# Unused matmuls during the first attention batch, a projection moved into the head pairs, and two casts moved to ScalarE, in a fused attention and MLP kernel

## The chip, the cores and the metric

The kernel runs on one core of one Trainium2 chip. The metric is the device time in microseconds (us) of one execution. Six executions of the kernel before had a median of 781.19 us (779.12 to 784.26).

Five engines appear in the profile, each with its own list of instructions, and they work side by side: in a span of 777.3 us PE was busy for 708.0 us and DVE for 336.0. PE is TensorE, which multiplies matrices. PEld is PE's loading of weights. DVE is VectorE, ACT is ScalarE, and POOL is GpSimd, which here mostly issues the loads from memory (DMA; 126 of its 140 instructions in the kernel before). The traces of that kernel show instructions that wait for what they read (0.74 us for `av` matmuls at 65.29) and for the buffer that they write (0.74 us for scores at 72.67, until the exponential before had read it). What stood behind a waiting instruction in its list waited too; the traces below show this for DVE (9.93 us).

## The reference

```python
# batch 8, heads 12, sequence 448, head_dim 64, d_model 768, rank 32
q_n = q / (norm(q, axis=-1) + 1e-6)
k_n = k / (norm(k, axis=-1) + 1e-6)
attn = softmax(q_n @ k_n.T / tau)            # tau = 0.1
x = heads_merged(attn @ v)                   # (8, 448, 768)
xt = x.transpose(0, 2, 1)
u = x + (xt @ U @ V).transpose(0, 2, 1)      # = (I + U V).T applied along the sequence
out = u + relu(u @ w_ch1) @ w_ch2            # w_ch1 768 x 3072, w_ch2 3072 x 768
```

## The kernel before

Work is organised by batch. `emit_attention(b)` loads and normalises q and k, then goes through six pairs of heads. `emit_mlp(b)` projects with `I + UV` (`pu`), then does the two large products `ph` (24 blocks of 6 matmuls) and `pc` (6 blocks of 24), transposes back (`po`) and stores. The program lists attention(0), attention(1), mlp(0), attention(2), mlp(1) and so on. The build turns that into one fixed order of instructions for each engine. In the middle of the run this order puts the matmuls of the MLP between those of the next attention, so PE has something to do (for 84.92 of 87.17 us in the period shown below). During attention(0) there is no MLP work yet.

The parts that matter here, cut:

```python
nc.vector.tensor_copy(out=u_nat_bf, in_=u_nat)     # two small casts, on DVE
...
nc.vector.tensor_copy(out=v_bf, in_=v_nat)
...
def emit_attention(b):
    ...                                   # 12 loads on the POOL queue: q (4), k (4), v (4)
    for w_, src, sc in ((0, q_bf, tau_f), (1, k_bf, 1.0)):
        for t in range(NT):               # NT = 4
            nc.vector.tensor_tensor(out=sq, in0=src[:, t], in1=src[:, t], op=ALU.mult)
            nc.vector.reduce_sum(out=ssq[:, w_, t], in_=sq, axis=mybir.AxisListType.X)
        nc.scalar.activation(out=nrm[:, w_], in_=ssq[:, w_], func=AF.Sqrt,
                             bias=sqrt_bias[:PT], scale=sc * sc)
        nc.vector.reciprocal(out=rcp[:, w_], in_=nrm[:, w_])
        ...                               # four multiplies on DVE: src *= rcp
    for p in range(NP):                   # NP = 6 pairs of heads
        ...                               # transposes of q and k into tp_ps; copy to tp_sb
        for jt in range(NT):
            sc_ps = psum.tile([PT, 2, 512], F32, name="sc_ps", tag="sc", bufs=1)
            ...                           # two score matmuls
            ex = apool.tile([PT, 2, S], BF16, name="ex", bufs=5)
            nc.scalar.activation(out=ex, in_=sc_ps[:, :, :S], func=AF.Exp)
        for hh in range(2):
            ...                           # av: 16 matmuls ex x v into av_ps (tag "av", bufs=2)
            ...                           # DVE: x = av / row sum
        for _ in range(3):                # 3 of the 30 weight loads, on the POOL queue
            ...
def emit_mlp(b):
    for cc in range(NC):
        pu = psum.tile([128, S], F32, name="pu", tag="mm", bufs=3)
        ...                               # 4 matmuls x x (I + UV); copy to uT
    ...                                   # ph -> relu, pc + uT -> oT, po -> ost -> out
```

There is one score buffer, so a score matmul has to wait until the exponential of the previous one has read it (0.92 us for each exponential; steps of 1.69 us in the slow attention(0) of the kernel before, at 71 to 74 us). I call the time from one score to the next a step; a pair has four.

## Time and profile before

| stage of the profiled run (span 777.3 us) | start, us | what limits it |
|---|---|---|
| load and normalise batch 0 | 0 | loads |
| attention(0), alone | 28 | slow array, score and exponential in turn, one stop for a load |
| attention(1) with `ph` of batch 0 | 100.50 | PE |
| `pc` of batch 0; from here about 86.5 us per batch | 156.57 | PE |
| last batch and tail | 708 | PE |

The head of the profile page gives each engine's busy time, then the busy tenths in 40 equal slices of the span (9 means 90% or more), then the share of each engine in the chain of work that ended last:

```profile
PE 708.0 (91%) x5000; PEld 388.8 (50%) x5000; DVE 336.0 (43%) x620; ACT 310.4 (40%) x399; POOL 108.5 (14%) x140
...
PE   1547799999999999999999999999999999999995
...
PEclk9999999999999999999999999999999999999998
DMA  9999983772099029342198029522000010002002
```

PE is the bottleneck, but only from the sixth slice on. Two thirds of PE's idle time, 46 of 69 us, lie in the first five slices, that is, the first 100 us. A mean of 91% hides that.

From the chain of waits in order of time (start, duration, what; all in us):

```profile
50.85 7.61 DMA q_bf<-in_q_dram
...
156.57 27.24 PE pc L220 x144
...
243.50 27.24 PE pc L220 x144
...
708.19 3.31 PE pu L192 x16
711.50 27.24 PE ph L206 x144
738.74 27.25 PE pc L220 x144
```

The starts of `pc` are a ruler. From one to the next is one batch, 86.93 us here. The load of q at 50.85 is on the chain because something had to stop for it. The stretch table shows how tight a period is, and how tight the start is not. Its columns are the stretch and its length, the busy time and count of PE, PEld, DVE, ACT and POOL, the granted clock, the DMA share and GB/s:

```profile
330.74:417.91 87.17, 84.92 (x625) 46.46 (x624) 43.52 (x80) 36.72 (x46) 11.44 (x13) 1.00 0.46 40
60.00:84.00 24.00, 19.19 (x108) 11.10 (x108) 17.01 (x31) 15.03 (x18) 13.96 (x21) 1.00 2.14 155
```

Now the start, instruction by instruction, from PE's timeline (start, duration, engine, line, operation, output<-inputs, shapes, count, and in brackets the idle time before and what ended it):

```profile
48.26 0.62 PE L147 MATMUL sc_ps<-tp_sb 64*112 64x448 bf16 x2
...
59.43 0.56 PE L192 MATMUL pu<-pt_sb,x 112*128 112x448 bf16 x1 [10.06 <-DVE x L170]
...
65.29 2.64 PE L162 MATMUL av_ps<-v_sb,ex 112*112 112x65 bf16 x26 [0.74 <-ACT ex L154]
...
104.58 1.70 PE L206 MATMUL ph<-uT,w 128*128 128x448 bf16 x4
...
109.26 1.11 PE L206 MATMUL ph<-uT,w 128*128 128x448 bf16 x5
110.28 1.53 PE L162 MATMUL av_ps<-v_sb,ex 112*112 112x65 bf16 x26
```

The same 26 `av` matmuls take 2.64 us at 65.29 and 1.53 us at 110.28. The array ran slow throughout attention(0), although the clock row shows 9 everywhere: from 60 to 84 us PE was busy for 19.19 of 24 us, and two scores took 0.62 us there. It became fast in the dense `ph` matmuls, about 4 us after they begin: they start at 104.58, and from 108.81 on two scores take 0.40 us. And PE stood still for 10.06 us. DVE's timeline shows why:

```profile
58.48 0.56 DVE L119 TENSOR_TENSOR sq<-q_bf 112x768 bf16<-112x768 bf16 x1 [9.93 <-DMA q_bf<-in_q_dram]
58.96 0.42 DVE L170 TENSOR_TENSOR x<-av_ps,rs 112x256 bf16<-112x256 f32 x1
```

The multiply that PE needed (`x`) had its inputs long before. But a square of batch 1's q stood ahead of it in DVE's queue, and that square waited for its load.

### The profile page before, as it was taken

The page shows a single profiled execution, that of the slowest core. Times are in us where ns is not written, and L with a number is a line of the kernel's source. Part 1 is how long each engine was busy: PE and PEld are TensorE (multiplying, and loading weights), DVE is VectorE, ACT ScalarE, POOL GpSimd, SP SyncE. Part 2 cuts the span into 40 slices and gives each one's busy share as a digit, 9 for nine tenths or more (in the row PEclk, how much of TensorE's full clock was granted, in tenths as well). Part 3 has the DMA queues.
Part 4 walks back from the last instruction along what each step waited for, and adds up shares of the span by engine and source line. Part 5 has one row for each costly group of instructions (what it writes and reads, how often), then busy time and mean ns, then how long its engine had stood idle before and what let it go on. Part 6 is the DMA issues. An engine that isn't in the chain of part 4 may idle for free.

```text
span 777.3 us, 11607 instructions
## 1 busy us (share of the span) xinstructions
PE 708.0 (91%) x5000; PEld 388.8 (50%) x5000; DVE 336.0 (43%) x620; ACT 310.4 (40%) x399; POOL 108.5 (14%) x140
## 2 busy tenths in 40 slices
PE   1547799999999999999999999999999999999995
PEld 0324455555555554555545555555555555554552
DVE  7418665933484155913484156813430153111011
ACT  2325557613563065603563056603552155303401
POOL 6355422110122003100122003100000000000000
PEclk9999999999999999999999999999999999999998
DMA  9999983772099029342198029522000010002002
GB/s 114 184 200 147 134 36 26 48 36 71 3 70 36 1 72 72 23 14 72 8 66 36 1 72 72 30 7 72 1 2 1 21 51 1 1 1 72 1 0 72
DMA packets 139539, 37.82 MB, mean 49 GB/s; under 512 B 132032, under 2 KB 135136, under 8 KB 139488
## 3 DMA queue, kind: packets, MB, share of 16 engines
q0 software_dynamic: 134880, 25.96, 48.7%
q1 hardware_dynamic: 4608, 11.13, 4.6%
q8 instruction: 39, 0.64, 0.4%
q14 instruction: 12, 0.10, 0.0%
HBM read 52.02 MB, written 11.01 MB: 81 GB/s over the span
## 4 chain that ended last, share of the span: by engine, by line
PE 76%; DMA 10%; ACT 6%; DVE 3%; POOL 2%; issue 2%; SPq 0%; ACTq 0%; POOLq 0%; DVEq 0%
PE pc L220 28%; PE ph L206 22%; PE av_ps L162 11%; PE sc_ps L147 7%; PE pu L192 4%; DMA q_bf<-in_q_dram 4%; DMA w<-in_moe_w_ch_dram 3%; ACT ex L154 3%; DMA v_sb<-in_v_dram 1%; POOL q_bf L106 1%; ACT L154 1%; PE tp_ps L137 1%; PE po L233 1%; PE tp_ps L135 1%; DVE ssq L120 1%
## 5 line engine op out<-in xcount | busy, mean ns | idle before, releaser
L206 PE MATMUL ph<-uT,w 128*128 128x448 bf16 x1152 | 245.7, 354 | 0.0
L154 ACT ACTIVATE ex<-sc_ps 112x896 bf16<-112x896 f32 x192 | 176.0, 917 | 154.6 <-PE sc_ps L147 152.6
L220 PE MATMUL pc<-relu,w 128*128 128x448 bf16 x1152 | 219.2, 352 | 0.0
L220 PEld LDWEIGHTS <-w 128*128 128x128 bf16 x1152 | 112.7, 98 | 105.2
L206 PEld LDWEIGHTS <-w 128*128 128x128 bf16 x1152 | 105.8, 100 | 88.9 <-issue 10.9
L227 DVE TENSOR_TENSOR oT<-pc,uT 128x448 bf16<-128x448 f32 x48 | 30.0, 624 | 239.5 <-PE pc L220 239.5
L162 PE MATMUL av_ps<-v_sb,ex 112*112 112x65 bf16 x1536 | 125.2, 228 | 8.6 <-DVE x L170 5.7
L162 PEld LDWEIGHTS <-ex 112*112 112x112 bf16 x1536 | 102.7, 141 | 47.4 <-issue 32.5
L236 ACT CAST ost<-po 112x768 f32<-112x768 bf16 x17 | 13.6, 798 | 225.4 <-PE po L233 221.3
L147 PE MATMUL sc_ps<-tp_sb 64*112 64x448 bf16 x384 | 82.2, 420 | 8.4 <-ACT ex L154 7.3
L213 ACT ACTIVATE relu<-ph 128x448 bf16<-128x448 f32 x120 | 65.1, 542 | 49.2 <-PE ph L206 49.1
L213 DVE TENSOR_SCALAR relu<-ph 128x448 bf16<-128x448 f32 x72 | 44.6, 619 | 42.4 <-PE ph L206 41.8
L192 PE MATMUL pu<-pt_sb,x 112*128 112x448 bf16 x192 | 50.5, 380 | 11.6 <-DVE x L170 10.2
L106 POOL DMA_DIRECT2D q_bf<-in_q_dram x32 | 30.0, 944 | 221.0 <-PE ph L206 199.4
L147 PEld LDWEIGHTS <-tp_sb 64*112 64x112 bf16 x384 | 28.2, 129 | 63.9 <-issue 58.1
L120 DVE TENSOR_REDUCE ssq<-sq 112x12 f32<-112x768 bf16 x64 | 59.2, 939 | 0.3
L110 POOL DMA_DIRECT2D v_sb<-in_v_dram x32 | 29.8, 937 | 107.2 <-issue 92.8
L140 DVE COPY tp_sb<-tp_ps 128x896 bf16<-128x896 bf16 x39 | 24.3, 623 | 46.4 <-PE sc_ps L147 32.8
L137 PE MATMUL tp_ps<-ident,k_bf 112*128 112x112 bf16 x192 | 31.3, 229 | 11.7 <-DVE k_bf L125 11.7
L170 DVE TENSOR_TENSOR x<-av_ps,rs 112x256 bf16<-112x256 f32 x96 | 39.6, 418 | 1.8
L135 PE MATMUL tp_ps<-ident,q_bf 112*128 112x112 bf16 x192 | 31.0, 227 | 9.8 <-DVE q_bf L125 5.6
L169 DVE RECIPROCAL rs<-av_ps 112x4 f32<-112x4 f32 x96 | 17.3, 180 | 45.4 <-PE av_ps L162 44.5
(37 smaller groups left out, 338.6 us busy)
## 6 DMA issues: line engine op xcount, KB each, us to landing
out_dram<-ost SPq DMA_DIRECT2D x32, 336.0 KB, 3.0
q_bf<-in_q_dram POOLq DMA_DIRECT2D x32, 168.0 KB, 5.4
k_bf<-in_k_dram POOLq DMA_DIRECT2D x32, 168.0 KB, 6.5
v_sb<-in_v_dram POOLq DMA_DIRECT2D x32, 168.0 KB, 6.6
w<-in_moe_w_ch_dram POOLq DMA_DIRECT2D x6, 768.0 KB, 13.0
w<-in_moe_w_ch_dram POOLq DMA_DIRECT2D x24, 192.0 KB, 7.6
u_nat<-in_moe_U_dram SPq DMA_DIRECT2D x1, 56.0 KB, 2.0
v_nat<-in_moe_V_dram SPq DMA_DIRECT2D x1, 56.0 KB, 2.4
```

Source lines behind the costliest of these rows:

```text
L106: nc.gpsimd.dma_start(out=q_bf[:, t], in_=qr[:, t])
L120: nc.vector.reduce_sum(out=ssq[:, w_, t], in_=sq, axis=mybir.AxisListType.X)
L135: nc.tensor.transpose(tp_ps[:, 0, t * PT:(t + 1) * PT], q_bf[:, t, 2 * p:2 * p + 2, :], ident[:PT, :PT])
L137: nc.tensor.transpose(tp_ps[:, 1, t * PT:(t + 1) * PT], k_bf[:, t, 2 * p:2 * p + 2, :], ident[:PT, :PT])
L147: nc.tensor.matmul(sc_ps[:, hh, :S], tp_sb[base:base + 64, 1, jt * PT:(jt + 1) * PT], tp_sb[base:base + 64, 0, :], start=True, stop=True,)
L154: nc.scalar.activation(out=ex, in_=sc_ps[:, :, :S], func=AF.Exp)
L162: nc.tensor.matmul(av_ps[:, ic, :], aw[jt][:, hh, ic * PT:(ic + 1) * PT], v_sb[:, jt, h, :], start=(jt == 0), stop=(jt == NT - 1),)
L170: nc.vector.tensor_tensor(out=xt[:, :, h, :], in0=av_ps[:, :, 1:], in1=rs[:, :, None].to_broadcast([PT, NT, D]), op=ALU.mult,)
L192: nc.tensor.matmul(pu, xt[:, t, 2 * cc:2 * cc + 2, :], pt_sb[t], start=(t == 0), stop=(t == NT - 1),)
L206: nc.tensor.matmul(ph, w1_sb[cc][:, fc * 128:(fc + 1) * 128], uT[cc], start=(cc == 0), stop=(cc == NC - 1),)
L213: nc.any.tensor_scalar_max(out=rl, in0=ph, scalar1=0.0)
L220: nc.tensor.matmul(pc, w2_sb[fc][:, cc * 128:(cc + 1) * 128], relu[fc], start=(fc == 0), stop=(fc == NF - 1),)
```

## The change

The intent is to win back the start and the batch changes. Unused matmuls (`dm`) in attention(0) are to keep the array fast. `pu` moves from the head of the MLP into each pair of heads, where it uses the `av` buffers instead of the `mm` buffers. Two small casts go from DVE to ACT, and `ex` gets a sixth buffer. The diff, cut to its core (the rest splits `emit_attention` into a prologue and a function per pair; the order of calls is the same):

```diff
-    nc.vector.tensor_copy(out=u_nat_bf, in_=u_nat)
+    nc.scalar.copy(out=u_nat_bf, in_=u_nat)
...
-    nc.vector.tensor_copy(out=v_bf, in_=v_nat)
+    nc.scalar.copy(out=v_bf, in_=v_nat)
...
+            if b == 0 and jt > 0:
+                dm = psum.tile([PT, S], F32, name="dm", tag="mm", bufs=3)
+                for _ in range(5):
+                    nc.tensor.matmul(dm, aw[-1][:, 0, :PT], aw[-1][:, 1, :], start=True, stop=True)
-                ex = apool.tile([PT, 2, S], BF16, name="ex", bufs=5)
+            ex = apool.tile([PT, 2, S], BF16, name="ex", bufs=6)
...
+        pu = psum.tile([128, S], F32, name="pu", tag="av", bufs=2)      # at the end of each pair
+        for t in range(NT):
+            nc.tensor.matmul(pu, xp[:, t, :, :], pt_sb[t], start=(t == 0), stop=(t == NT - 1))
+        ut = mpool.tile([128, S], BF16, name=f"uT_{p}", bufs=3)
+        nc.any.tensor_copy(out=ut, in_=pu)
...
-            pu = psum.tile([128, S], F32, name="pu", tag="mm", bufs=3)  # at the start of the MLP
-            ...
-            ut = mpool.tile([128, S], BF16, name=f"uT_{cc}", bufs=1)
```

More of the change, by code (lines that the diff above doesn't have):

```diff
@@ L41 @@
     tau_f = float(tau)
-    assert S == NT * PT and C == NC * 128 and F == NF * 128 and H % 2 == 0
+    assert S == NT * PT and C == NC * 128 and F == NF * 128 and H % 2 == 0 and NC == NP
     const = ctx.enter_context(tc.tile_pool(name="const", bufs=1))
     wpool = ctx.enter_context(tc.tile_pool(name="wpool", bufs=1))
-    xpool = ctx.enter_context(tc.tile_pool(name="xpool", bufs=1))
     apool = ctx.enter_context(tc.tile_pool(name="apool", bufs=1))
@@ L91, with emit_attention_prologue @@
     w_loads = w_loads[::-1]
-    x_sb = {}
-    def emit_attention(b):
-        xt = xpool.tile([PT, NT, H, D], BF16, name=f"x_{b % 2}", bufs=1)
-        x_sb[b] = xt
+    batch_ctx = {}
+    uT_all = {b: [None] * NP for b in range(B)}
+    def emit_attention_prologue(b):
         q_bf = apool.tile([PT, NT, H, D], BF16, name="q_bf", bufs=2)
@@ L130, in emit_attention @@
                 )
-        for p in range(NP):
-            tp_ps = psum.tile([128, 2, S], BF16, name="tp_ps", tag="tp", bufs=1)
-            for t in range(NT):
-                nc.tensor.transpose(tp_ps[:, 0, t * PT:(t + 1) * PT],
-                                    q_bf[:, t, 2 * p:2 * p + 2, :], ident[:PT, :PT])
-                nc.tensor.transpose(tp_ps[:, 1, t * PT:(t + 1) * PT],
-                                    k_bf[:, t, 2 * p:2 * p + 2, :], ident[:PT, :PT])
-            tp_sb = apool.tile([128, 2, S], BF16, name="tp_sb", bufs=2)
-            nc.any.tensor_copy(out=tp_sb, in_=tp_ps)
-            aw = []
-            for jt in range(NT):
-                sc_ps = psum.tile([PT, 2, 512], F32, name="sc_ps", tag="sc", bufs=1)
-                for hh in range(2):
-                    base = hh * 64
+        batch_ctx[b] = (q_bf, k_bf, v_sb)
@@ new lines, in emit_attention_pair @@
+    def emit_attention_pair(b, p):
+        q_bf, k_bf, v_sb = batch_ctx[b]
+        tp_ps = psum.tile([128, 2, S], BF16, name="tp_ps", tag="tp", bufs=1)
+        for t in range(NT):
+            nc.tensor.transpose(tp_ps[:, 0, t * PT:(t + 1) * PT],
+                                q_bf[:, t, 2 * p:2 * p + 2, :], ident[:PT, :PT])
+            nc.tensor.transpose(tp_ps[:, 1, t * PT:(t + 1) * PT],
+                                k_bf[:, t, 2 * p:2 * p + 2, :], ident[:PT, :PT])
+        tp_sb = apool.tile([128, 2, S], BF16, name="tp_sb", bufs=2)
+        nc.any.tensor_copy(out=tp_sb, in_=tp_ps)
+        aw = []
+        for jt in range(NT):
+            sc_ps = psum.tile([PT, 2, 512], F32, name="sc_ps", tag="sc", bufs=1)
+            for hh in range(2):
+                base = hh * 64
+                nc.tensor.matmul(
+                    sc_ps[:, hh, :S],
+                    tp_sb[base:base + 64, 1, jt * PT:(jt + 1) * PT],
+                    tp_sb[base:base + 64, 0, :],
+                    start=True, stop=True,
+                )
+            if b == 0 and jt > 0:
[3 more added lines that the diff above has]
+            ex = apool.tile([PT, 2, S], BF16, name="ex", bufs=6)
+            nc.scalar.activation(out=ex, in_=sc_ps[:, :, :S], func=AF.Exp)
+            aw.append(ex)
+        xp = apool.tile([PT, NT, 2, D], BF16, name="xp", bufs=3)
+        for hh in range(2):
+            h = 2 * p + hh
+            av_ps = psum.tile([PT, NT, D + 1], F32, name="av_ps", tag="av", bufs=2)
+            for ic in range(NT):
+                for jt in range(NT):
@@ L147, in emit_attention @@
                     nc.tensor.matmul(
-                        sc_ps[:, hh, :S],
-                        tp_sb[base:base + 64, 1, jt * PT:(jt + 1) * PT],
-                        tp_sb[base:base + 64, 0, :],
-                        start=True, stop=True,
-                    )
-                ex = apool.tile([PT, 2, S], BF16, name="ex", bufs=5)
-                nc.scalar.activation(out=ex, in_=sc_ps[:, :, :S], func=AF.Exp)
-                aw.append(ex)
-            for hh in range(2):
-                h = 2 * p + hh
-                av_ps = psum.tile([PT, NT, D + 1], F32, name="av_ps", tag="av", bufs=2)
-                for ic in range(NT):
-                    for jt in range(NT):
-                        nc.tensor.matmul(
-                            av_ps[:, ic, :],
-                            aw[jt][:, hh, ic * PT:(ic + 1) * PT],
-                            v_sb[:, jt, h, :],
-                            start=(jt == 0), stop=(jt == NT - 1),
-                        )
-                rs = apool.tile([PT, NT], F32, name="rs", bufs=3)
-                nc.vector.reciprocal(out=rs, in_=av_ps[:, :, 0])
-                nc.vector.tensor_tensor(
-                    out=xt[:, :, h, :],
-                    in0=av_ps[:, :, 1:],
-                    in1=rs[:, :, None].to_broadcast([PT, NT, D]),
-                    op=ALU.mult,
-                )
@@ L177, in emit_attention @@
-            for _ in range(3):
-                if w_loads:
-                    wt, wsrc = w_loads.pop()
-                    nc.gpsimd.dma_start(out=wt, in_=wsrc)
-        if b == 1:
-            while w_loads:
+                        av_ps[:, ic, :],
+                        aw[jt][:, hh, ic * PT:(ic + 1) * PT],
+                        v_sb[:, jt, h, :],
+                        start=(jt == 0), stop=(jt == NT - 1),
+                    )
+            rs = apool.tile([PT, NT], F32, name="rs", bufs=3)
@@ new lines, in emit_attention_pair @@
+            nc.vector.reciprocal(out=rs, in_=av_ps[:, :, 0])
+            nc.vector.tensor_tensor(
+                out=xp[:, :, hh, :],
+                in0=av_ps[:, :, 1:],
+                in1=rs[:, :, None].to_broadcast([PT, NT, D]),
+                op=ALU.mult,
+            )
+        pu = psum.tile([128, S], F32, name="pu", tag="av", bufs=2)
+        for t in range(NT):
+            nc.tensor.matmul(
+                pu,
+                xp[:, t, :, :],
+                pt_sb[t],
+                start=(t == 0), stop=(t == NT - 1),
+            )
@@ L183, in emit_attention @@
+        ut = mpool.tile([128, S], BF16, name=f"uT_{p}", bufs=3)
+        nc.any.tensor_copy(out=ut, in_=pu)
+        uT_all[b][p] = ut
+        for _ in range(3):
+            if w_loads:
                 wt, wsrc = w_loads.pop()
@@ L186, in emit_mlp @@
     def emit_mlp(b):
-        xt = x_sb.pop(b)
-        uT = []
-        for cc in range(NC):
-            pu = psum.tile([128, S], F32, name="pu", tag="mm", bufs=3)
-            for t in range(NT):
-                nc.tensor.matmul(
-                    pu,
-                    xt[:, t, 2 * cc:2 * cc + 2, :],
-                    pt_sb[t],
-                    start=(t == 0), stop=(t == NT - 1),
-                )
-            ut = mpool.tile([128, S], BF16, name=f"uT_{cc}", bufs=1)
-            nc.any.tensor_copy(out=ut, in_=pu)
-            uT.append(ut)
+        del batch_ctx[b]
+        uT = uT_all.pop(b)
         relu = []
@@ L237, in emit_mlp, with flush_w_loads @@
             nc.sync.dma_start(out=out[b, t * PT:(t + 1) * PT, :], in_=ost)
-    LAG = min(1, B - 1) if B > 1 else 1
-    if B == 1:
-        emit_attention(0)
+    def flush_w_loads():
         while w_loads:
@@ L244 @@
             nc.gpsimd.dma_start(out=wt, in_=wsrc)
+    if B == 1:
+        emit_attention_prologue(0)
+        for p in range(NP):
+            emit_attention_pair(0, p)
+        flush_w_loads()
         emit_mlp(0)
     else:
-        for step in range(B + LAG):
-            if step < B:
-                emit_attention(step)
-            if step >= LAG:
-                emit_mlp(step - LAG)
+        for b in range(B):
+            emit_attention_prologue(b)
+            for p in range(NP):
+                emit_attention_pair(b, p)
+            if b == 1:
+                flush_w_loads()
+            if b >= 1:
+                emit_mlp(b - 1)
+        emit_mlp(B - 1)
 _INS = ['q', 'k', 'v', 'tau', 'moe_U', 'moe_V', 'moe_w_ch1', 'moe_w_ch2']
```

## The prediction

> **What bounds the kernel now.** The page gives PE 708.0 of 777.3 us, 91%; the chain of waits is 76% PE. Two regimes hide in that average.
>
> - Steady state. In the chain, the second MLP product (pc) starts at 156.57, 243.50, 330.74, 417.91, 504.52, 590.57 and 675.68 us: about 86.5 us per batch. By the stretch table PE is busy 84.9 of 87.2 us. The list of waits shows only 0.6 to 2.2 us of PE idle per period (av on x 0.8 to 1.5; transposes on tp_sb 0.5; po on ost 0.2). Matmuls stream at 27.24 us / 144 = 189 ns. There is little to win.
> - Start. pc of batch 0 starts only at 156.57. From 28.0 to 100.5 us attention(0) runs alone: 72.5 us for six pairs, against about 7.4 us per pair later. By the PE timeline, three things cost this: (a) the array is slow: a pu matmul takes 374 ns, a score pair 0.62 instead of 0.40 us, 26 av matmuls 2.64 instead of 1.5 us. It turns fast only at 108.8 us, 4 us after the dense ph matmuls begin. [...]the granted-clock column already reads 1.00 there. (b) PE idles 10.06 us before 59.43: an x multiply on DVE stands behind batch 1's first square, which waits for q until 58.46, the load being queued after 18 weight loads. (c) One score buffer: matmul and exp (0.92 us) alternate, 1.69 us per step.
>
> **What the change does.**
>
> 1. 18 x 5 = 90 unused matmuls in attention(0): 17 us at 189 ns, 34 us slow. In the fast state five (0.95 us) fit under one exp: the steady state runs five ph matmuls per step at 1.49 us. In the slow state they stretch a step from 1.69 to about 2.5 us, but then fill PE for several us, so I expect the fast state within the first pair, lost in the DMA stall, regained after it.
> 2. pu moves from the MLP's start into each pair (buffers of av instead of mm). Count unchanged; the scheduler already ran batch 0's pu per pair. It removes the pu wait chain at batch changes (0.7 us each) and in the last batch, where 8.4 us pass between pc(6) and ph(7) for 4.5 us of pu and about 1.5 of po. Risk: a third user of two av buffers and a new x-to-pu wait in the attention chain.
> 3. Two casts go to ACT (0.6 us off DVE), and a sixth ex buffer: nothing on the chain.
>
> **Sum.** Attention(0): p0 and p1 get faster, but the stall until 58.5 us remains, only longer, since weights and q are DMA-bound (DMA 9 tenths until 60 us). After it, 41 us become about 31: pairs of 7.5 us, with DVE (batch 1's normalisation, about 20 us) nearly full. Gain 10 us. Ph(0) starts fast: 3 us. Batch changes: 3 us. Last batch: 2 us. New stalls: -2 us. Total about 16 us: 765 us.
>
> Predicted 765 us, 80% range 751 to 777. Faster by over 2%: 0.52; within 2%: 0.45; slower: 0.03.
>
> **What would show it.** av x26 at about 1.5 us before 60 us; pc(0) starting near 143 (plus 4.5 us for pu(1) now done before it: 148); a PE gap of 10 to 15 us ending near 59; the period still 86 to 87 us; ph(7) directly after po(6).
>
> **What would make it wrong.** The dummies never trigger the fast state (up to 20 us slower); DVE order changes so that the stall vanishes (10 us more gain) or grows; pu waiting on x stalls PE in every pair (42 pairs x 0.3 us).

The sum: 10 + 3 + 3 + 2 − 2 = 16 us, and from 781 us that gives 765. That the unused matmuls would bring the fast state was my estimate from one observation, the array that became fast 4 us into the dense `ph` matmuls. That the stall would lose it again was a guess: no trace had shown that by then.

## The result

The kernel after had a median of 771.85 us (768.18 to 773.31, 8 runs), against 779.44 us (777.37 to 784.26, 16 runs) for the kernel before in the same rounds. The ratio is 0.9888, with a 95% interval of 0.9867 to 0.9909. A ratio here is the mean time of one kernel's fast runs over that of the other's of the same rounds, so it is not quite the ratio of the medians. Later (e0_after in the table below) the kernel after got 0.9877 (0.9857 to 0.9897). All outputs are right. So the change wins a little over 1%. The time is inside the predicted range, but the gain is half of the one predicted. It counts as "within 2%", where I had put slightly more weight on "faster by over 2%".

The head of the page after (span 771.5 us):

```profile
PE 711.1 (92%) x5090; PEld 388.3 (50%) x5090; DVE 329.2 (43%) x606; ACT 313.2 (41%) x413; POOL 108.5 (14%) x140
...
PE   1548899999999999999999999999999999999995
...
PEclk9978799999999999999999999999999999999998
```

The chain of waits after:

```profile
51.50 7.60 DMA q_bf<-in_q_dram
...
157.66 27.24 PE pc L220 x144
...
244.37 27.24 PE pc L220 x144
...
708.13 25.13 PE ph L206 x132
733.26 27.25 PE pc L220 x144
```

This is the first surprise: `pc` of batch 0 starts at 157.66 us, 1.1 us *later* than before. About 4.5 us of that is `pu` of batch 1, which now lies ahead of it. So on equal work the start gained only 3.4 us. In the last batch `pc` follows the previous `pc` by 57.85 us instead of 63.06. Of these 5.2 us, the same 4.5 are `pu` that has moved away, so 0.7 us are won.

A period of the steady state, and the two stretches after the stop:

```profile
331.14:417.43 86.29, 85.22 (x626) 46.05 (x624) 41.50 (x77) 38.14 (x50) 11.21 (x14) 1.00 0.47 41
60.00:84.00 24.00, 21.34 (x151) 12.71 (x152) 19.76 (x36) 15.05 (x17) 14.16 (x22) 0.91 2.00 146
84.00:96.00 12.00, 11.04 (x59) 6.89 (x59) 9.81 (x18) 3.79 (x6) 3.32 (x4) 0.57 1.88 127
```

PE's timeline after, in attention(0):

```profile
31.29 2.11 PE L155 MATMUL dm<-ex 112*112 112x448 bf16 x5
...
33.90 1.15 PE L155 MATMUL dm<-ex 112*112 112x448 bf16 x5
...
36.33 1.78 PE L166 MATMUL av_ps<-v_sb,ex 112*112 112x65 bf16 x30
...
60.08 1.67 PE L183 MATMUL pu<-pt_sb,xp 112*128 112x448 bf16 x4 [13.42 <-DVE xp L174]
...
79.17 0.40 PE L146 MATMUL sc_ps<-tp_sb 64*112 64x448 bf16 x2 [0.91 <-ACT ex L157]
...
84.83 1.98 PE L155 MATMUL dm<-ex 112*112 112x448 bf16 x5
...
100.00 0.40 PE L146 MATMUL sc_ps<-tp_sb 64*112 64x448 bf16 x2
```

Five unused matmuls take 2.11 us at 31.29 and 1.15 us at 33.90: the array became fast within the first pair. PE's last wait before that had ended at 29.90, 4.0 us earlier. Then PE stops until 60.08, now for 13.42 us, because it was early for an event that hardly moved (the square starts at 59.12 us, before at 58.48):

```profile
59.12 0.56 DVE L116 TENSOR_TENSOR sq<-q_bf 112x768 bf16<-112x768 bf16 x1 [13.08 <-DMA q_bf<-in_q_dram]
59.60 0.42 DVE L174 TENSOR_TENSOR xp<-av_ps,rs 112x256 bf16<-112x256 f32 x1
```

During the stop the granted clock fell to half (0.50 from 49 to 60 us). At 84.83 five `dm` take 1.98 us again, so the array was slow a second time (granted clock 0.55 from 84.5 to 90 us, 0.50 from 90 to 95), although no wait of PE since the stop had been longer than 0.91 us. The first scores of attention(1) are at 100.00 us; before they were at 100.50. From the end of the stop to there it took 39.9 us (100.00 − 60.08), before 41.1 us (100.50 − 59.43). The prediction had said 31.

Where did the predicted 31 us go? In pairs that run fast and unhindered in this trace, a step takes 1.47 us, and the one step in four that carries most of the `av` matmuls takes 3.08 us. The 15 steps from the score at 61.68 to that at 100.00 would take 11 × 1.47 + 4 × 3.08 = 28.5 us. They took 38.3. Going through the starts of the score matmuls one by one, I put the 9.8 us of excess down as follows (an estimate from the trace: each step's excess goes to what PE did or waited for in it). The array was still slow just after the stop: 1.2 us. Two steps held a square root on ACT, with waits on `ex`, `xp` and `k_bf`: 3.0 us. A `pu` lay inside a step: 0.7 us. The second slow spell, until about 95 us: 4.9 us, although one of its steps also holds a `pu`. What sets off that spell is not shown (see e9).

ACT's timeline shows one of those square roots:

```profile
80.59 1.28 ACT L118 ACT_TABLE_LOAD   x1
81.89 0.33 ACT L118 ACTIVATE nrm<-ssq,sqrt_bias 112x48 f32<-112x48 f32 x1
82.24 1.28 ACT L157 ACT_TABLE_LOAD   x1
83.53 0.92 ACT L157 ACTIVATE ex<-sc_ps 112x896 bf16<-112x896 f32 x1
```

In this trace ACT loads a function table (1.28 us) before the square root of 0.33 us and another (1.28 us) before the exponential after it: from 80.59 to 83.53, 2.9 us, no exponential runs. The square root starts 0.02 us after its load ends (80.59 + 1.28, then 81.89). With a single score buffer PE soon has to wait: the scores at 84.50 waited 0.47 us for the exponential at 83.53, and they came 3.17 us after the scores before them. There were as many table loads before the change (31 in each of the two traces, of 1283 ns each). There, too, one of the loads lies on the chain of waits (1.28 us at 83.60).

### The profile page after: what moved, and what is told of

Read it like the earlier page. It is cut to its first block, busy times and chain, and to the rows that moved or that the text cites. A ratio compares the mean times of both kernels' runs of the same rounds, so it can differ in the third digit from the quotient of the medians.

```text
span 771.5 us, 11752 instructions
## 1 busy us (share of the span) xinstructions
PE 711.1 (92%) x5090; PEld 388.3 (50%) x5090; DVE 329.2 (43%) x606; ACT 313.2 (41%) x413; POOL 108.5 (14%) x140
## 4 chain that ended last, share of the span: by engine, by line
PE 80%; DMA 11%; ACT 3%; DVE 2%; POOL 2%; issue 1%; SPq 0%; ACTq 0%; POOLq 0%; DVEq 0%
PE pc L220 28%; PE ph L206 24%; PE av_ps L166 11%; PE sc_ps L146 7%; DMA q_bf<-in_q_dram 5%; PE pu L183 4%; DMA w<-in_moe_w_ch_dram 4%; PE dm L155 2%; DMA out_dram<-ost 1%; DMA v_sb<-in_v_dram 1%; POOL q_bf L103 1%; PE tp_ps L136 1%; PE tp_ps L134 1%; ACT ost L236 1%; PE po L233 1%
## 5 line engine op out<-in xcount | busy, mean ns | idle before, releaser
L206 PE MATMUL ph<-uT,w 128*128 128x448 bf16 x1152 | 255.3, 353 | 0.8 <-ACT relu L213 0.6
L166 PE MATMUL av_ps<-v_sb,ex 112*112 112x65 bf16 x1536 | 118.9, 220 | 0.2
L166 PEld LDWEIGHTS <-ex 112*112 112x112 bf16 x1536 | 96.4, 133 | 37.6 <-issue 24.7
L213 DVE TENSOR_SCALAR relu<-ph 128x448 bf16<-128x448 f32 x96 | 59.7, 622 | 67.4 <-PE ph L206 66.3
L146 PE MATMUL sc_ps<-tp_sb 64*112 64x448 bf16 x384 | 77.5, 399 | 3.8 <-ACT ex L157 2.8
L213 ACT ACTIVATE relu<-ph 128x448 bf16<-128x448 f32 x96 | 52.0, 542 | 32.2 <-PE ph L206 31.7
L183 PE MATMUL pu<-pt_sb,xp 112*128 112x448 bf16 x192 | 45.8, 362 | 19.4 <-DVE xp L174 19.4
L190 ACT CAST uT<-pu 128x448 bf16<-128x448 f32 x46 | 24.5, 532 | 47.9 <-PE pu L183 47.9
L174 DVE TENSOR_TENSOR xp<-av_ps,rs 112x256 bf16<-112x256 f32 x96 | 40.0, 422 | 2.2
L183 PEld LDWEIGHTS <-xp 112*128 112x128 bf16 x192 | 17.9, 99 | 39.1 <-DVE xp L174 24.2
```

The source lines that it names most:

```text
L146: nc.tensor.matmul(sc_ps[:, hh, :S], tp_sb[base:base + 64, 1, jt * PT:(jt + 1) * PT], tp_sb[base:base + 64, 0, :], start=True, stop=True,)
L166: nc.tensor.matmul(av_ps[:, ic, :], aw[jt][:, hh, ic * PT:(ic + 1) * PT], v_sb[:, jt, h, :], start=(jt == 0), stop=(jt == NT - 1),)
L174: nc.vector.tensor_tensor(out=xp[:, :, hh, :], in0=av_ps[:, :, 1:], in1=rs[:, :, None].to_broadcast([PT, NT, D]), op=ALU.mult,)
L183: nc.tensor.matmul(pu, xp[:, t, :, :], pt_sb[t], start=(t == 0), stop=(t == NT - 1),)
L206: nc.tensor.matmul(ph, w1_sb[cc][:, fc * 128:(fc + 1) * 128], uT[cc], start=(cc == 0), stop=(cc == NC - 1),)
L213: nc.any.tensor_scalar_max(out=rl, in0=ph, scalar1=0.0)
```

## The experiments

My theory after the result was: the dummies work, but speed gained ahead of the stop is lost in the stop, and after it the next limits take over (table loads, DVE). Its first rival was that the dummies do nothing useful, because the matmuls they add cost what they win. A second rival came up later: the small edits that I had called harmless carry the result. The expectations, quoted as they were written before each run, put theory and rivals in the terms of that run. Medians are given with the median of the kernel before; the intervals are 95%.

| run | median, us | before, us | ratio | interval |
|---|---|---|---|---|
| e1_no_dm | 773.16 | 779.33 | 0.9919 | 0.9905 to 0.9933 |
| e2_before_dm | 782.55 | 779.33 | 1.0038 | 1.0015 to 1.0062 |
| e3_early | 778.72 | 779.33 | 1.0000 | 0.9984 to 1.0016 |
| e4_early_no_dm | 774.43 | 779.33 | 0.9937 | 0.9919 to 0.9956 |
| e7_tied | 767.80 | 778.58 | 0.9859 | 0.9836 to 0.9882 |
| e8_tied_no_dm | 774.87 | 778.58 | 0.9952 | 0.9932 to 0.9973 |
| e0_after | 769.28 | 778.79 | 0.9877 | 0.9857 to 0.9897 |
| e11_small_undone | 779.85 | 778.79 | 1.0003 | 0.9971 to 1.0036 |
| e9_merged | 764.39 | 778.79 | 0.9822 | 0.9803 to 0.9841 |
| e10_tied_merged | 768.60 | 778.79 | 0.9878 | 0.9844 to 0.9911 |
| e13_casts_dve | 780.07 | 780.12 | 1.0001 | 0.9971 to 1.0031 |
| e14_merged_no_dm | 772.28 | 780.12 | 0.9884 | 0.9862 to 0.9907 |

### The dummies alone, taken away and added (e1, e2)

e1 is the kernel after without the dummies. e2 is the kernel before with nothing but the dummies.

```diff
 # e1: from the kernel after
-            if b == 0 and jt > 0:
-                dm = psum.tile([PT, S], F32, name="dm", tag="mm", bufs=3)
-                for _ in range(5):
-                    nc.tensor.matmul(dm, aw[-1][:, 0, :PT], aw[-1][:, 1, :], start=True, stop=True)
 # e2: the same four lines added to the kernel before, ahead of its ex tile
```

> The new kernel without the 90 unused matmuls: the fusion, the casts and the sixth ex buffer alone. Theory (the trace of the changed kernel): the change's 8 us are about half the fast ph(0) start that the unused matmuls buy, half the batch changes and the last batch that the fusion buys; so this one lies near 775 us, 0.994 to 0.996 of the kernel before, with the array slow (av x26 at 2.6 us) until about 105 us and a PE gap of about 10 us ending near 59. Rival 1, all of the gain is the clock: 1.00. Rival 2, all of it is the fusion: 0.989.

> The kernel before with the 90 unused matmuls alone. Theory: about 3 us faster than before (776 us, 0.996), because the wait of DVE for q of batch 1 still ends near 59 us and the array turns slow in it and again near 84 us. Rival 1 (all of the gain is the clock): 0.989. Rival 2 (all is the fusion): 1.00 or slower, since 17 us of matmuls are added.

Without the dummies the kernel after keeps most of its gain: 0.9919, against 0.9888 and 0.9877 with them. The 0.994 to 0.996 that I had expected was a miss. The dummies are worth 0.3 to 0.4%, some 3 us; these are different calls, and the first of the two intervals with them touches that of e1. Added to the kernel before they make it *slower* by 0.38%; the 776 us that I had expected there was a miss. Its profiled run was the fastest of its six (778.19 us, `pc` of batch 0 at 154.12), and the slower ones have a lower mean clock (0.965 in the one of 785.55 us), so I have no trace of what slowed them. This stays open.

The trace of e1 shows a cost of the dummies that I had not counted. They take the `mm` buffers in attention(0), and without them the build finds useful work to put there:

```profile
60.81 1.31 PE L202 MATMUL ph<-uT,w 128*128 128x448 bf16 x3
```

With the dummies, the first `ph` matmul of the kernel after comes at 100.73 us. What e1 lacks is the clock: its granted clock is 0.50 from 84 to 96 us, and 0.61 in the 12 us on either side of that.

### Moving the load that stops DVE (e3, e4)

e3 issues batch 1's loads of q and k ahead of the weights. e4 does so without the dummies.

```diff
+    def emit_qk_loads(b):
+        ...                               # the q and k loads, cut out of the prologue
         for b in range(B):
             emit_attention_prologue(b)
+            if b == 0:
+                emit_qk_loads(1)          # ahead of the weight loads
             for p in range(NP):
```

> The new kernel with the q and k loads of batch 1 issued before the weight loads; nothing else. Theory: the predicted 10 us were swallowed by the wait for q of batch 1, which stops PE for 13.4 us and lets the clock fall; with q there early the gap ending near 60 us goes, the array stays fast through attention(0), its six pairs take 45 to 52 us instead of 72, and the total falls by 13 to 20 us against the new kernel, to 752 to 759 us (0.965 to 0.974 of before). Rival (the wait only hides a second limit, DVE's normalisation of batch 1, or the later weights): the gap goes, but the total falls by less than 6 us.

> The same early loads without the unused matmuls. Theory: the gap goes but the array stays slow, pairs of 10.5 us, so 63 to 66 us for attention(0): 6 to 9 us faster than the kernel with neither, 766 to 769 us; the unused matmuls are then worth 10 to 15 us, not 3. Rival (the unused matmuls are worth the same 3 us with or without the wait): within 4 us of the run with both.

Both theories missed. The rival of e3, a second limit behind the wait, fits better, but the total did not fall at all: it rose. The stop at 59 us disappeared, and in e3 the pairs of attention(0) began about 7.7 us apart from 51.56 us on, close to the 7.5 us of an unhindered pair (3 × 1.47 + 3.08). But then DVE met the same obstacle one batch further on:

```profile
86.50 0.56 DVE L124 TENSOR_TENSOR sq<-q_bf 112x768 bf16<-112x768 bf16 x1 [18.75 <-DMA q_bf<-in_q_dram]
...
91.33 0.62 DVE L147 COPY tp_sb<-tp_ps 128x896 bf16<-128x896 bf16 x1
```

```profile
92.00 0.25 PE L142 MATMUL tp_ps<-ident,q_bf 112*128 112x112 bf16 x1 [16.89 <-DVE tp_sb L147]
```

The first fence is DVE's timeline, the second PE's. The wait did not go away, it moved from batch 1's q to batch 2's and got longer. The weights still come in through the same queue: in e3's POOL timeline all 30 weight loads are issued from 27.98 us on, and batch 2's q follows at 78.02. With the dummies (1.0000) this is slower than without (0.9937).

### Spreading the weight loads (e7, e8)

e7 issues q, k and v of batch 1 and the six large weight tiles first. Then it ties each remaining weight load to a pair of heads: a one-column copy from that pair's `xp` into the weight tile makes the load wait for the pair (in e7's POOL timeline two such copies at 51.76 had waited 9.69 us for `xp`, and their loads follow at 52.24). Two loads follow each of the first four pairs of batch 0, four each in batch 1. e8 is the same without the dummies.

```diff
-        for _ in range(3):
-            if w_loads:
+        for _ in range(2 if b == 0 else 4):
+            if w_loads and p < 4:
                 wt, wsrc = w_loads.pop()
+                nc.gpsimd.tensor_copy(out=wt[:PT, 0:1], in_=xp[:, 0, 0, 0:1])
                 nc.gpsimd.dma_start(out=wt, in_=wsrc)
```

> The new kernel with a load order that keeps q of the next batch ahead of the second MLP matrix: q, k, v of batch 1 and the six tiles of the first matrix at once; each tile of the second matrix waits, through a one-column copy, for a pair of attention(0) or attention(1), so that q and k of batch 2 are not queued behind all of them. Theory (the start is bound by the order in which the loads land, because DVE's queue stops at the first square whose q is missing): the early-load run only moved the wait from batch 1's q to batch 2's; here neither is longer than 5 us, attention(1) starts near 80 us instead of 100, the second product of batch 0 near 137 instead of 157.7, and the total is 750 to 758 us, 0.962 to 0.972 of before. Rival (the loads' sum, not their order, is the limit, or DVE is): another wait takes its place and attention(1) still starts later than 92 us; total above 765 us.

> The same load order without the unused matmuls. Theory: with no wait for loads left, the slow array sets the pace: attention(0) takes pairs of about 10.5 us, attention(1) starts near 92 us, the total is 8 to 14 us above the run with them. Rival (the unused matmuls are worth nothing, since they take the fill's place): the two within 3 us.

```profile
68.54 0.56 DVE L129 TENSOR_TENSOR sq<-q_bf 112x768 bf16<-112x768 bf16 x1 [6.50 <-DMA q_bf<-in_q_dram]
```

In DVE's timeline the longest wait for q is now 6.50 us, and attention(1) starts at 93.74 us instead of 100.00. At 0.9859 this is 767.80 us, well short of the 750 to 758 that the theory expected, so the stop was not the only thing that held the start. In attention(0) PE's score matmuls now wait 5.3 us for exponentials; the longest of these waits (2.31 us) stands behind a square root's tables (loads of 1.28 us at 43.87 and 45.52). The array was also slow twice: the mean granted clock is 0.74 from 47 to 60 us and 0.86 from 60 to 84, where five `dm` take 2.11 us at 76.11. The dummies are worth 0.9% here (0.9859 against 0.9952), two to three times what they are worth in the kernel after. The 7.1 us are just under the 8 to 14 that e8's theory expected, and they speak against the rival that the dummies do nothing: they paid here, where less else stopped PE (from 47 to 60 us it was busy for 12.22 of 13 us, in the kernel after for 0.00). The other rival quoted above, that attention(1) would not start before 92 us and the time stay above 765, held.

### One square root per batch (e9, e10, e14)

e9 is the kernel after with one square root for q and k together from batch 1 on, so that ACT changes tables once per batch and not twice (from 60 to 95 us ACT's timeline shows one square root with its two loads, at 71.98 and 74.12; in the kernel after it shows two, with loads at 67.30 and 69.43 and at 80.59 and 82.24). The factor tau moves into the exponential.

```diff
-        for w_, src, sc in ((0, q_bf, tau_f), (1, k_bf, 1.0)):
-            ...                           # 4 squares and sums; Sqrt with scale sc * sc; 4 multiplies
+        pairs = ((0, q_bf), (1, k_bf))
+        for group in ((pairs[:1], pairs[1:]) if b == 0 else (pairs,)):
+            ...                           # 4 or 8 squares and sums; one Sqrt, scale 1; 4 or 8 multiplies
-            nc.scalar.activation(out=ex, in_=sc_ps[:, :, :S], func=AF.Exp)
+            nc.scalar.activation(out=ex, in_=sc_ps[:, :, :S], func=AF.Exp, scale=1.0 / tau_f)
```

e10 adds the tied loads of e7. e14 is e9 without the dummies. e0_after is the kernel after as it is, a control.

> The changed kernel again, unaltered, as the control of this call: 0.987 to 0.991 of the kernel before.

> The changed kernel with one square root per batch instead of two from batch 1 on (the factor tau moves into exp), so that ACT swaps its function tables once per batch and not twice. Theory: inside attention(0) each swap pair (1.28 + 0.33 + 1.28 us on ACT) sits in the alternation of score matmul and exp[...]; one pair less gives 2 to 5 us, 0.983 to 0.987 of before. Rival: the start is bound by q's arrival and DVE alone, the swap hides in it: within 1 us of the control.

> The tied load order with the one square root per batch, as a version that should beat both kernels. Theory: with the loads out of the way attention(0) carries four swap pairs (batches 1 and 2, two each), of which two go: 4 to 8 us less than the tied order alone, 760 to 764 us, 0.976 to 0.981 of before. Rival: less than 2 us, because DVE's two normalisations (20 us each) set the pace.

> One square root per batch, without the unused matmuls. Theory: where the wait for q is unchanged[...], the unused matmuls keep attention(0) fast between the waits, so without them 4 to 8 us are lost against the run with both (0.982): 0.988 to 0.992 of before. Rival: they are worth no more than the 2 to 3 us that they were in the changed kernel: 0.982 to 0.986.

e9 is the best version: 764.39 us, 0.9822, with only 1.6 us between its fastest and slowest run. It beats both kernels, the kernel after by 4.9 us. From e9's profile, the clock row of the page, and then PE's timeline:

```profile
PEclk9989999999999999999999999999999999999998
```

```profile
56.95 1.67 PE L187 MATMUL pu<-pt_sb,xp 112*128 112x448 bf16 x4 [10.57 <-DVE xp L178]
...
92.06 0.40 PE L150 MATMUL sc_ps<-tp_sb 64*112 64x448 bf16 x2
```

About 5 us after the stop the clock is full (0.98 from 60 to 72 us, then 1.00), and in the clock row it stays so to the last slice: the second slow spell is gone, and from the end of the stop to attention(1) it takes 35.1 us instead of the 39.9 of the kernel after (38.1 in the control's trace, which also has a second slow spell, of about 4 us). Three cautions. In this profiled run the stop also ended 3.2 us earlier than in the control's, because the early loads came in sooner: POOL's wait for v of batch 0 already ends 2.1 us earlier (20.83 against 22.93 us). The edit is not likely to be the reason, since e14, which has it too (without the dummies), waits until 22.85 and ends its stop at 59.04. From the end of the stop to `pc` of batch 0, e9 is 2.1 us faster than the control (93.1 against 95.2), and over the six periods after that 2.1 us more (515.98 against 518.05). Next, merging also changes the order of DVE's work and of PE's, so I cannot say how much is the tables alone. And the second slow spell need not come from the tables. In the control, the same kernel as the kernel after, it begins before this square root's table load, as PE's timeline and then ACT's show:

```profile
80.69 2.12 PE L155 MATMUL dm<-ex 112*112 112x448 bf16 x5
```

```profile
81.79 1.28 ACT L118 ACT_TABLE_LOAD   x1
```

In e9, PE was busy for only 1.83 us of the 3.5 from 83.5 to 87 and the clock stayed full. So what sets the spell off stays open.

e14 gives 0.9884, as expected: the dummies are worth 0.6% in the best version (on different chips). e10 missed: 0.9878 where 0.976 to 0.981 was expected. Its runs scatter from 765.27 to 774.00 us. The two remedies do not add; why is open.

### The parts I had called harmless (e11, e13)

e11 puts the two casts back on DVE and `ex` back to five buffers. e13 puts back only the casts.

```diff
-    nc.scalar.copy(out=u_nat_bf, in_=u_nat)
+    nc.vector.tensor_copy(out=u_nat_bf, in_=u_nat)
-    nc.scalar.copy(out=v_bf, in_=v_nat)
+    nc.vector.tensor_copy(out=v_bf, in_=v_nat)
-            ex = apool.tile([PT, 2, S], BF16, name="ex", bufs=6)      # e11 only
+            ex = apool.tile([PT, 2, S], BF16, name="ex", bufs=5)      # e11 only
```

> The changed kernel with its two small parts undone (the two casts of U and V back on DVE, five ex buffers). Theory, as predicted: they lie off the chain of waits, so the ratio stays within 0.002 of the control's. Rival: the sixth ex buffer lets exp run ahead of av and is worth over 2 us.

> The changed kernel with only the two casts of U and V back on DVE (six ex buffers stay). With five ex buffers and the casts on ACT the instruction order of PE, DVE and ACT is the same as the changed kernel's; with the casts on DVE it is not: on DVE the first square of batch 2 then stands ahead of the k multiply of batch 1. Theory: the casts alone make the loss of the run with both small parts undone, through that order: 0.998 to 1.003 of before, PE idle for 5 to 7 us on k_bf of batch 1 near 86 us. Rival: the ex buffer made it; 0.986 to 0.991.

Both lose the whole gain: 1.0003 and 1.0001. Two casts of together 0.6 us, in the first microseconds, are worth 1.2% of the kernel (1.0001 against 0.9877), nearly 10 us. The second rival holds. The casts take too little time themselves to explain that. What differs is what the build chose afterwards. Built again and compared with the kernel after, e13 has another instruction at 680 of the 10188 places of PE's list (matmuls and weight loads), and DVE's list is in another order too. The build also divided the work between DVE and ACT anew: e13's page counts 604 instructions on DVE and 415 on ACT, the kernel after's 606 and 413, although two casts went to DVE; on balance four ReLUs, which the program leaves to either engine (`nc.any`), went the other way. No run separates the order from this division. With five `ex` buffers and nothing else changed, the built order of the work is the same on PE, DVE and ACT as with six (built, not run), so the sixth buffer changes no order. One place where the new order costs time, from e13's DVE timeline, and then from PE's:

```profile
85.16 0.56 DVE L116 TENSOR_TENSOR sq<-q_bf 112x768 bf16<-112x768 bf16 x1 [3.49 <-DMA q_bf<-in_q_dram]
85.64 3.56 DVE L122 TENSOR_TENSOR k_bf<-k_bf,rcp 112x768 bf16<-112x768 bf16 x4
```

```profile
86.64 0.27 PE L136 MATMUL tp_ps<-ident,k_bf 112*128 112x112 bf16 x1 [4.69 <-DVE k_bf L122]
```

It is the same pattern a third time. The multiply of batch 1's k, which PE needs next, now stands behind a square of *batch 2's* q, whose load has not come in. PE waits 4.69 us, a little less than the 5 to 7 that I had expected. In the kernel after, that wait is 0.76 us:

```profile
83.76 0.22 PE L136 MATMUL tp_ps<-ident,k_bf 112*128 112x112 bf16 x1 [0.76 <-DVE k_bf L122]
```

`pc` of batch 0 starts at 160.56 us in e13 and at 155.37 in the control: 5.2 of the 5.5 us between the spans of these two profiled runs (775.0 and 769.5) are lost before it. Against the other profile of the kernel after (157.66) it is only 2.9. The medians lie further apart, because e13's profiled run is one of its faster ones (778.38 us, median 780.07) and the control's is its slowest (771.51, median 769.28).

The granted clock of all the runs shows more. In each of the eight kernels with dummies, the runs with the lower mean clock tend to be the slower ones (correlations of −0.72 to −0.99 within a kernel). The six runs of e13 have a mean clock of 0.977 on average, as have those of e11; those of the control have 0.986. By my estimate (0.009 × 770 us / 0.5) that is some 14 us more at half clock in e13. So the loss goes with a longer slow array as well as with the wait on k. That what the build chose prolongs the slow array is likely, but not shown. Whether moving the casts alone would also help the kernel before was not run, and neither was the moved `pu` alone, without casts and dummies.

## Why the prediction was right or wrong

- *"There is little to win" in the steady state, with a period of 86 to 87 us: right.* From `pc` of batch 0 to that of batch 6 took 519.11 us before and 517.75 after, so 1.4 us were won. The prediction had 3 us for batch changes less 2 for new stalls, which is 1.
- *"The fast state within the first pair, lost in the DMA stall, regained after it": right, but incomplete.* Fast from 33.90 us, half clock in the stop (0.50), fast again about 5 us after it. Then it was lost a second time from 84.5 to about 95 us (0.55, then 0.50), which I had not foreseen.
- *"The stall until 58.5 us remains, only longer": right.* It grew from 10.06 to 13.42 us and ended at 60.08.
- *"After it, 41 us become about 31 … Gain 10 us": this is the step that failed.* It took 39.9 us. The gain in the start of attention(1) was 0.5 us. I had let the pairs run at the steady pace of 7.5 us as soon as the array was fast. In its place the trace shows a second slow spell (about 4.9 us of excess), square roots whose table loads and k multiplies hold up the score steps (3.0), the slow array just after the stop (1.2) and `pu` in a step (0.7). This division is an estimate from one trace. e9 merges the two square roots, has no second slow spell in its trace, and is 4.9 us faster over the whole kernel, but it also reorders the work, so the share of each cause is not shown.
- *"Ph(0) starts fast: 3 us": right.* From attention(1)'s first score to `pc` of batch 0 took 56.07 us before. After, it took 57.66 with 4.5 us of `pu` in it, so 53.2.
- *"Last batch: 2 us": too high.* It was 0.7 us plus 0.3 in the tail (38.24 against 38.56 us after the start of the last `pc`).
- *"Two casts … and a sixth ex buffer: nothing on the chain": wrong for the casts.* Without them there is no gain (e13: 1.0001). I had costed what the two instructions take and not what the build then does with the others.
- *The sum.* Between the two profiled runs 3.4 us came from the start, 1.4 from the periods, 0.7 from the last batch and 0.3 from the tail: 5.8 us, which is 777.3 less 771.5. The prediction had 16. The measured time lay in the range, but in part by luck, since the range was wide (751 to 777): the largest term did not appear, and a term set to zero decides whether there is any gain.
- *The risk that `pu` waits on `xp`* came out small. In the period shown it is one wait of 0.6 us, where before there were two waits of `av` on `x` (1.4 us in all).

## What to carry to other kernels

Here a stop for a load was felt through an engine that worked in order: DVE waited 9.93 us for batch 1's q, and PE 10.06 us for the multiply behind it (13.42 us after the change, 16.89 us in e3). So look for what stands *ahead* of the needed instruction in its queue, and which batch that belongs to. Speed won ahead of such a stop only lengthened it here (10.06 us to 13.42), and removing it in one place (e3) may move it to the next; so follow the chain to the next fixed event before counting a gain. An edit that costs nothing by itself can still make the build reorder hundreds of instructions, so test "harmless" parts of a change alone before crediting the intended part. And unused matmuls, kept for the clock, were worth from −0.6% (e3 against e4) to +0.9% (e7 against e8) here; that this depends on what else stopped PE is my reading of these runs.
